# Parting two accumulations, moving a table add to TensorE, and joining maxima over two banks, in an attention and gated MLP kernel

## The chip, the cores and the metric

The kernel runs on one core of one Trainium2 chip. Its time is the device time of one execution in microseconds (us), as a median of runs. A profile of one execution gives each engine's instructions: TensorE (PE, and PEld for its weight loads), VectorE (DVE), ScalarE (ACT), GpSimd (POOL) and the DMA issues of SyncE (SP).

## The reference

Windowed attention with a linear bias by distance, for 8 batches of 8 heads, 576 positions and 64 columns a head, followed by a gated MLP over the 512 joined columns:

```
scores = scale * q @ k.T + slope[h] * -abs(i - j)    # kept where 0 <= i - j < 128, else -1e9
attn   = softmax(scores);  x = attn @ v
h = relu(x @ w_in);  u, v = h[:, :512], h[:, 512:]
v_n = layer_norm(v);  v_s = w_spatial @ v_n + b_spatial
out = (u * v_s) @ w_out
```

## The kernel before

Heads are taken in pairs (p = 0 to 3). The program first lists its operations (`plan.add`, and `plan.either` where two engines may do one), each with what it reads and writes. The string `PLACES` gives each operation a rank, three hexadecimal digits, by which each engine's queue is ordered; the instructions are then written out in that order, and every engine works through its queue in order.

**Batch 0 and half of batch 1** go through `turned`. PE makes first scores in two groups (tiles 0, 1, 2 and tiles 3, 4), each in two of four PSUM banks, `s`, one bank a head. DVE adds the bias table and takes each row's maximum in one instruction for each head and tile (line 765), ten for a pair. The maxima are turned by PE (line 783) into a bank `m`, and copied to `row`. Then PE makes the scores again, transposed, with table and maxima added by products with an identity and with ones (line 795); ACT takes exponentials (line 815); PE multiplies by v (line 824) into the two banks `x`; line 851 and 852 make the reciprocal of the sums; line 856 (DVE) or 862 (ACT) scales; line 869 turns the result back into `x`; lines 464 and 881 write it as a high and a low half, `xt`. The next pair's line 824 needs both `x` banks free.

**The MLP** of a batch (`gated`) is made of units of PE work that take the two banks `m` in turn: five v units (lines 1083 and 1105, twelve products each over four chunks of the contraction, chunk c being pair c's `xt`), then u, mixing (line 1155) and output units. A v unit is followed by a layer norm on DVE and POOL. The weights come as 64-bit floats in loads and DVE operations in the first 100 us; `mixing_weights` prepares the spatial weights, with a product for their largest column sum that takes both banks `m` (line 528), and comes in the list before the v units. `column_scale` is the helper for that product.

**Idle products.** Where the planner's model finds PE idle in the first 110 us, `emit` writes products whose result nobody reads (`fill`, line 391), 192 columns into the second `x` bank.

```
fills = int((now - idle) / (82 * (1 + low))) + 2 * (now < 30000)
```

Of the kernel before, what the change touches and what calls it, by code (L numbers as in the profile page):

```python
# [16 lines left out]
ALU = mybir.AluOpType  # L17
# [4 lines left out]
def _as_f32(bits):  # L22
# [9 lines left out]
    "00000500300200a01601a00600400c09c1e900902000701901b04800b04a03b05f03506005308005608200100d01101303102e05505904304201501c01d02202502a02802d"  # L32
    "03203403903d09d04404104505c06204d05105705e06c07207507818d1991a018b1a41a600800e00f01201001401701e01802302601f02402902c03702102702b03003302f"
    "03a03804704e05205d06306504f05b06606a07103603e04004603f04904c06803c04b05005a05805406406707607b07e08508908d07c08408809209306106906e06b06f074"
    "07707a06d07007308308707908c08e0980a20af0b80bc0c00a40b00b30b50b907d08108a0990970910a30a00c70cc0d20d60de0e40d00d90db0e00e207f09009609ba9a086"
    "0940aa0ba09e0c60ac0ae0e30b10c20bf0bb0b70c90c11430cf0cb0d70dc0e60eb0ef0f20f81cd11c12315415c13f14410b0f70c50ca0ce0d40da1021050e90f60fa0fd101"
    "10710f1130ff10c11011511b11e12b1300ea0f00fc0fe10310d10e10a11811d12112a12f13413611211712512919413513912e13212613a13e14715015716216913313b141"
    "14514b14f15315915e16816314615214d15b13c14014815117617f15816015f16a16717416f17917e19316116416c17317b1851781871801881a81b518919519f1a71cc1ae"
    "1a91b91bf1b41ba1c91c31d519019e1ad1b819d1b21aa1b71c01c71b61c11bc1cb1f020e1c61d61ed2051d11de1ef1e31f220720c1ec1fe20b1fa20d22920a21f224227221"
    "23324722c23d25223e24c25a25425e34f25927034708b08f0f30f509509a09f0a50ab0b60a70bd0c40e80ec0ee1f60f90a10a80b40a90a60ad0b20be0c30c80cd0d30d50d1"  # L40
    "0dd0e10fb10010611612012d10911111912212c0d80ed0df0e70e50f10f410410811411a12412711f12813113814a14c1551ea20218a19119b1f420613713d15617214915d"
    "16b18315a17516e17a16617714216d17d14e16517018217117c1841921961981ac1b31a11a519719a19c1a21db1d41dd1bd1ce1cf1da1d21e21af1d31f818118618e1d71a3"
    "1d91e71e81c81dc18c1b018f1ab1b11e51e61d81e11d01df1e01e41eb1ee1f11fb1fc2011f51fd1f91ff1f31f721320f21621121721b21e21821c21521a234200208219240"
    "24423f2421bb2041c22091c521d1be23b24825626c26f2774891c420321022021422622a22f23023822222822e23522d23122522b21222323223923c24125025324924f246"
    "24d24e25124324b26226326725826126026426626825525b27c23623a24a25725d25c25f27926527627d28328c29129629927528528a28f29229729b29f2a52a92ac28029e"
    "2a02a42aa2b02b42b929c2b12d02e02e42e82eb2ed2a72bd2d52dc2e12e72e92ec36f2b82c42bf2cf2c92d72d32ee2db2fc2f130233633d2ff30a30631633933b31031e346"
    "34d31b32c32534535735b33035534c36239739a35936c3a53a936537739137237e3a83ab37a3893953833a23af38c3a63aa3ac3a73b33cf3ae3bd3dc3b73d13e63c23e049d"
    "3d83e94a21ca23726b27a26a27e26927227428727128627828927328426e28226d27f27b28b28e2902942982a32a62a12a229329529a29d2bb2ab2b32a82b22ad2b52b72bc"
    "2af2b62d224528128828d2c22d92c62e22c02c82cb2d62c52d12ca2d82c72da2cd2df2ce2dd2c12cc2de2e32c32d42e62ea2f62fb2ef2f22f92fd2f02f52f42f830d303309"
    "30530b30831130730f30130e3242ae2ba2be2e531733231533431a31f32832f32a33132232731831d31331932932d31432332632b31c32133533a34234834434b33e34133c"  # L50
    "33f34034336934e35334a35135235635035435c36e3802f32fe2fa30c30431230033333835d38e3933995e92f732032e33738d38f39039236636d35a35f360363374375371"
    "37336736b35e36136a37036436837637837b37c37d38237f38438538838738a38138639d39e3a139639f39839c39b3a33a03a43b634937938b3943b13c73bb3c43fc3e13f2"
    "40040340740a40c40f3f03fa3fe40b40e41041241441741a4193f541141341641841b41d41e40141c42542a43143743a43d41542242c42f43443843b4414b841f428426432"
    "42d43943644243e44e44645348a48e45145c4564644a04a646146c4a54a94674784714944a84aa47d4a34994ac4e74eb4a74b74ea4ee4b24c14cf4be4cd4f44f94c94d44e9"
    "4d14e05044d94f34f84fb4e34fa50a50051052f5085155335145325f851c5365fb3be3c03b93c83b03b83c93cd3c53ce3b23b53ba3c33bf3ca3c13c63bc3cc3d03d23d33d5"
    "3d43d73d63da3d93dd3db3de3ee3e53eb3e23e83e33ea3e43ed3e73ef3ff3583ad3b43cb4044083f83fb4064303fd42e3f44233f342040242b3f94244054273f7421409433"
    "3f642943543c43f44344444844044544a44c44744b45a45445f45245845745d45946045545b4703df3ec3f140d46947f46b48446a47247347546846f47447747647a481485"
    "47b48047947c47e48346646d48848b49149649a4a148f49249349849549b4bc48d49049c4a449749e4ad4c34b04c64d644945e44d46245046548248748c4af4e14fc501727"
    "44f46346e4864e54e84e44e64b44b64c44c84bf4c54ba4c04bb4c24cb4cc4b14b94b54bd4c74ca4ae4b34ce4d04d84de4d54dd4d24d74da4df4d34db4f24f14f74f64fe4fd"
    "4ff4ec4f04ef4f551249f4dc4e24ed51852250d51f54f53554655155655955d56056254254c55055e56156356556756a56b56d54856456656956c56e57057255456f575577"  # L60
    "57a57f58258556857357957b57d5805845875f657157657457c57858157e58658358e58a5935c35c959059a5955a45ca5ce59e5ae5d05d55a75b75b05c25d15d75be5cd5c7"
    "5d96146285d45f561962b5de5fe61d5f961261863160260d62361762c64762462e63363763263f64863d65666865566468766066e74466a68a74a50550b507511521523502"
    "50651d52051b51e50c51950950f50e51651351a52552652852b52752952a52d52e53152c53054053853b53753c53953e53a54153d5435524ab50351752455555754554754b"
    "58855b59254a58955858c54958f55c59655359154d58b54e58d55a5945975985a05a25a35a559d5a159959c59b59f5b85a95ac5ba5bf5b55bc5b25b95ad5af5d253453f544"
    "55f5c55e05c15e25bb5d65c45da5c65dd5cc5df5c05d85b15c85b65d35b35cb5db5e15b45cf5e45e65f05f45e75ea5e85ed5ec5ef5ee5f26075fd60160960e60460860660a"
    "6006036295a65bd5ab5e35eb5f35f15f75fc64564b67267789e5aa5a85dc5e563063962f63560f61361c62161661b61e62661a61f62262a62062761161560c61060560b62d"
    "63463663c63b64363a64063863e64264465164964c65365764f65264a64e64d65066f5fa5ff62564665c66c65a66668867468968b69169769c6a46a768e69b69f6ae6b26b5"
    "6b86bb6bd6be6c06986ab6b96bc6bf6c16c36c56a36c26c76c96cc6d06d56dc6b06c66ca6cd6d26d76de6e47606c46cb6c86d36ce6da6d86e16df6ec6e76f77307366f2701"
    "6fb70c73c74370571774b74e71072171a72974d75072574872d75478d79174f75f79079475a76a77676777479279777177b78f77778579578079b79f7a27887a17af7a77b5"
    "7d47ad7bb7dc7ba7d78987c27de89c67567665465865b65f67167365e66266366d66166b65966566967065d66767867a68468668068368268567c67f67e68169d694699696"  # L70
    "69a68c68f6926956906936ac64167967b67d6a86aa6a16a56b66e36a26d46a96d16b16d96b76e56b36dd6b46e06af6d66ad6db6a66cf6e86e96eb6ef6ed6f46ea6f16f06f9"
    "6f36f870d70470870b71270770a6fe70370970f72468d69e6a06ba72f73472e73270271171971c71571871d72071371671f72271b71e6ff70e72372670671472b731733739"
    "73573b73a73f73e74173773d76474674974274c74074775176e75576277c6e26e66ee6f66f56fa6fc70072a75878a7a37a89e96fd72872c73878b78e78978c75675c763769"
    "76676b75275776876d75b76175d76577077275975e76c76f77377578378677977e77878477d78277a78179d79679979c7a07987a579a79e7a47a67b774577f7877937c17c8"
    "7b67c67f67da7ec7f97fc8008038058087e97f37f780480780980b80d8108138127ee80a80c80f8118148168177fa81581f82682a83083383780e81b82382882d831836838"
    "8a481882181e82b82583282e83983584483c84987e88284684f84b85988b89085685d88f89685b86986288089189786e88d88589a8c48ce8928a08d48d889d8ae8bd8a68b7"
    "8e68ea8b18c18dd8ba8c98ed8c68e58e88eb8cf8e18ee8ec8f890b8f28fd9109069179e39139249e57b47be7b27b97a97ac7c37c77c07c47ae7b37c57c97b17bf7ab7b07b8"
    "7bc7cb7cc7d57d87d07d37cd7cf7ce7d17d27d67e77db7e37e27e87df7e47e07e67dd7e17f87537aa7bd7ca7eb7ed7fd7ff7f181c7fe8277f281a7ef81d7f081980282c7f5"
# [42 lines left out]
class Plan:  # L121
# [69 lines left out]
    def order(self, links, due, clocked, phase=0):  # L191
# [12 lines left out]
        while events or any(ready.values()):  # L204
# [8 lines left out]
            for e, heap in ready.items():  # L213
                if heap and free[e] <= now:
# [8 lines left out]
                    else:  # L223
# [1098 lines left out]
```

## Time and profile before

| | |
|---|---|
| median of 3 runs | 550.73 us (549.65 to 551.71) |
| profiled execution | 549.54 us, span 547.8 us, 1.7 us lie around the span |
| PE busy | 535.9 us, 98% of the span, idle products included |
| DVE busy | 450.1 us, 82% |
| ACT busy | 388.5 us, 71% |

A busy PE is not PE at its best: ends of products are modelled, and idle products count as busy. The share of an engine is an average over a start, in which loads, weights and the first batches are prepared, and a long steady part.

### The profile page before, as it was taken

How to read it: one execution, taken by the hardware profiler on the slowest of the kernel's cores; microseconds unless marked ns; L12 is line 12 of the kernel's file. 1: busy time of each engine (PE TensorE's matmuls, PEld its weight loads, DVE VectorE, ACT ScalarE, POOL GpSimd, SP SyncE). 2: the span in 40 equal slices, each digit the busy share in tenths (PEclk: the TensorE clock that was granted, in tenths of full speed). 3: DMA queues.
4: the chain of work that ended last, by engine and by line, in shares of the span. 5: the costliest groups of instructions: out<-in, count | busy, mean ns of one | idle time of the engine just before them, and what ended most of it. 6: DMA issues, size and time to landing. Idle time of an engine off the chain costs nothing.

```text
span 547.8 us, 19213 instructions
## 1 busy us (share of the span) xinstructions
PE 535.9 (98%) x7756; PEld 396.3 (72%) x7759; DVE 450.1 (82%) x1644; ACT 388.5 (71%) x1213; POOL 60.3 (11%) x124
## 2 busy tenths in 40 slices
PE   9898999999999999999999999999999999999997
PEld 7787577875588857886678757886678757784775
DVE  8877999999998899688995899779997699725540
ACT  7576798998987797568874898579877687423212
POOL 1020220202110002100310010100210011001000
PEclk9999999999999999999999999999999999999999
DMA  8869331389979975968478786869364774510002
GB/s 247 310 201 320 96 104 59 82 161 241 193 156 222 193 144 129 223 104 191 108 151 182 143 189 133 193 133 196 104 124 119 150 89 89 88 66 23 2 12 75
DMA packets 161405, 78.67 MB, mean 144 GB/s; under 512 B 124834, under 2 KB 155554, under 8 KB 161316
## 3 DMA queue, kind: packets, MB, share of 16 engines
q1 hardware_dynamic: 161316, 77.45, 62.8%
q8 instruction: 60, 0.98, 0.8%
q14 instruction: 29, 0.24, 0.1%
HBM read 37.13 MB, written 9.44 MB: 85 GB/s over the span
## 4 chain that ended last, share of the span: by engine, by line
PE 80%; DVE 11%; DMA 3%; ACT 2%; issue 1%; SPq 1%; POOL 1%; ACTq 0%; DVEq 0%; POOLq 0%
PE m L1155 20%; PE m L1187 16%; PE m L1134 15%; PE m L1083 10%; PE s L724 6%; PE x L998 6%; PE m L1105 2%; DMA out_dram<-o 1%; DMA vb<-in_v_dram 1%; PE x L824 1%; PE s L795 1%; PE x L391 1%; DVE st L1044 1%; DVE vt L1057 1%; DVE staged L1094 1%
## 5 line engine op out<-in xcount | busy, mean ns | idle before, releaser
L922 ACT ACTIVATE prob<-prob,stat 128x192 f32<-128x192 f32 (+1 forms) x260 | 109.2, 423 | 11.3 <-DVE stat L916 10.9
L1155 PE MATMUL m<-wsp,staged 128*128 128x288 f16 x768 | 112.8, 286 | 0.0
L1134 PE MATMUL m<-xt,win 128*128 128x288 f16 x768 | 100.2, 286 | 1.5 <-ACT vt L468 1.5
L1187 PE MATMUL m<-gs,wout 128*128 128x288 f16 x768 | 99.4, 286 | 0.0
L954 ACT ACTIVATE pq<-prob,stat 128x192 f16<-128x192 f32 (+1 forms) x260 | 88.1, 420 | 11.3 <-issue 3.7
L1134 PEld LDWEIGHTS <-win 128*128 128x128 f16 x768 | 74.9, 98 | 22.7 <-issue 2.9
L1155 PEld LDWEIGHTS <-staged 128*128 128x128 f16 x768 | 74.5, 98 | 21.0 <-issue 2.2
L959 DVE SCALAR_TENSOR_TENSOR pq<-prob,stat,pq 128x192 f16<-128x192 f32 (+1 forms) x260 | 87.0, 379 | 2.9 <-ACT pq L954 2.5
L1187 PEld LDWEIGHTS <-wout 128*128 128x128 f16 x768 | 74.3, 98 | 20.5 <-issue 2.0
L916 DVE CUSTOM_DVE_ANT_0 prob<-s,tab 128x192 f32<-128x192 f32 (+1 forms) x260 | 71.3, 318 | 20.0 <-PE s L724 19.8
L1083 PE MATMUL m<-win,xt 128*128 128x512 f16 x384 | 86.6, 379 | 0.8 <-ACT o L1193 0.8
L1083 PEld LDWEIGHTS <-xt 128*128 128x128 f16 x384 | 36.2, 98 | 46.1 <-issue 5.5
L1053 POOL TENSOR_TENSOR st<-st,nhalf 128x1 f32<-128x1 f32 (+1 forms) x40 | 29.7, 742 | 296.4 <-DVE st L1049 288.1
L724 PE MATMUL s<-qkraw 64*64 64x64 f32 (+1 forms) x1116 | 52.7, 313 | 0.0
L1163 DVE TENSOR_TENSOR u<-m,u 128x288 f32<-128x288 f32 x64 | 28.9, 451 | 28.4 <-PE m L1155 28.1
L922 ACT ACTIVATION_READ_ACCUMULATOR prob<-prob,stat 128x1 f32 (+1 forms) x260 | 49.4, 190 | 0.0
L468 ACT ACTIVATE u<-m 128x288 f32<-128x288 f32 x60 | 24.3, 405 | 30.4 <-PE m L1134 30.3
L1193 ACT ACTIVATE o<-m,am 128x288 f32<-128x288 f32 x32 | 15.9, 499 | 41.2 <-PE m L1187 31.0
L724 PEld LDWEIGHTS s<-qkraw 64*64 64x64 f32 x1116 | 40.8, 133 | 2.0 <-issue 1.2
L998 PEld LDWEIGHTS <-vh 128*64 128x64 f16 (+1 forms) x1664 | 34.4, 111 | 8.7 <-issue 7.2
L998 PE MATMUL x<-moved,vh 128*64 128x64 f16 (+1 forms) x1664 | 39.2, 196 | 0.0
L998 PE MATMUL x<-moved,vl 128*64 128x64 f16 (+1 forms) x832 | 37.5, 195 | 0.0
(167 smaller groups left out, 761.4 us busy)
## 6 DMA issues: line engine op xcount, KB each, us to landing
qkraw<-in_qk_dram SPq DMA_DIRECT2D x28, 576.0 KB, 4.2
vb<-in_v_dram SPq DMA_DIRECT2D x32, 320.0 KB, 6.0
out_dram<-o SPq DMA_DIRECT2D x64, 144.0 KB, 2.1
staged<-in_w_in_dram SPq DMA_DIRECT2D x8, 512.0 KB, 7.1
moved<-in_w_out_dram SPq DMA_DIRECT2D x4, 512.0 KB, 6.3
gw<-in_w_spT_dram SPq DMA_DIRECT2D x4, 288.0 KB, 6.0
moved<-pq SPq DMA_TRANSPOSE x52, 4.8
qkraw<-in_qk_dram SPq DMA_DIRECT2D x2, 320.0 KB, 5.2
```

The source lines that it names most:

```text
L724: nc.tensor.matmul(sc[j]()[out, at:at + k1 - k0], raw()[rows, 0, i * D:(i + 1) * D], raw()[rows, 1, k0:k1], start=True, stop=True, skip_gr ...
L916: nc.vector.tensor_tensor_reduce(pt(), sc[t][j]()[:m, SOFF[t]:SOFF[t] + n], tabs[h]()[:m, W - n:], -0.125, 3e38, ALU.add, ALU.min, st()[:m ...
L922: nc.scalar.activation(pt(), pt(), AF.Exp, bias=st()[:m, NM, j, t:t + 1], scale=-1.0, accum_out=st()[:m, SM, j, t:t + 1])
L954: nc.scalar.activation(pq[j]()[:m, 0, qs], prob[2 * (p % 2) + j]()[:m, cs], AF.Copy, scale=st()[:m, RC, j, t:t + 1])
L959: nc.vector.scalar_tensor_tensor(pq[j]()[:m, 1, qs], prob[2 * (p % 2) + j]()[:m, cs], st()[:m, RC, j, t:t + 1], pq[j]()[:m, 0, qs], ALU.mu ...
L998: nc.tensor.matmul(xp()[j * D:(j + 1) * D, x0:x0 + D], l()[rows, kt, j * D:(j + 1) * D], rhs, start=(i % 2, j) not in seen, stop=False, sk ...
L1053: nc.gpsimd.tensor_tensor(st()[:m, 11:12], st()[:m, 10:11], nhalf()[:m], ALU.pow)
L1083: nc.tensor.matmul(pt(), xt[c]()[:, X0[a] + t * P:X0[a] + (t + 1) * P], win()[:, c, w, DH:DF], start=(n == 0), stop=(n == 3 * NC_ - 1))
L1134: nc.tensor.matmul(pt()[:, :HS], win()[:, c, w, d * P:(d + 1) * P], xt[c]()[:, X0[a] + hf * HS:X0[a] + (hf + 1) * HS], start=(n == 0), sto ...
L1155: nc.tensor.matmul(pt()[:, :HS], l, r, start=(n == 0), stop=(n == len(ops) - 1))
L1163: nc.vector.tensor_tensor(u(), pt()[:, :HS], u(), ALU.mult)
L1187: nc.tensor.matmul(pt()[:, cs], wout()[:, d, w, e * P:(e + 1) * P], gs[d]()[:, a, cs], start=(n == 0), stop=(n == 3 * ND - 1))
```

## The change

Seven edits, and a new order string.

1. `v_unit` takes its contraction in parts. For the first two v units of batch 0 the parts are chunks 0 and 1, chunk 2, chunk 3, each an operation of its own with its own reads; the bank stays open between them.
2. For batch 0, `scored` adds the bias table to the first scores on PE, by a product of an identity with the table for each head and half tile (18 for a pair). DVE then takes plain maxima over both heads' banks at once, in three instructions for a pair: tile 0, tiles 1 and 2, tiles 3 and 4. For this the four `s` banks become one tensor. The maxima now come with the other sign, so `row` is multiplied by a new constant `less` (-1) in place of `ones`.
3. `mixing_weights` comes in the list after the first two v units, just before the third.
4. The bias row of the mixing weights is scaled with one instruction over two partitions, on DVE or ACT, and one on one partition, in place of three on one partition each.
5. The two DVE instructions of lines 851 and 852, and those of lines 1048 and 1049, become operations of their own.
6. Idle products: half as many after 5 us and no two extra ones, in the first bank of `x1`, `m1`, `m0` that the plan shows quiet; none where no bank is quiet.
7. `rest` takes two `s` banks instead of one where its tag is `s`. A constant `nident` is made; the branch that would use it, `LOWER`, has no members.

The diff, without the order string and the definitions of new constants:

```
-                                fills = int((now - idle) / (82 * (1 + low))) + 2 * (now < 30000)
+                                fills = int((now - idle) / ((82 if now < 5000 else 164) * (1 + low)))
...
+        for n, k, z, start, *_, fills in out:
+            if fills:
+                bank = next((b for b in FILLED if quiet(b, free, start)), None)
+                if bank or start < 5000:
+                    self.fill(fills, bank=bank or FILLED[0])
...
+    OPEN = (0, 2), (2, 3), (3, 4)
+    ADDED = [(0, p) for p in range(4)]
+    LOWER = []
...
-    plan.kept["s"] = [ps.tile([P, 4 * P], F32, name=f"s{k}") for k in range(4)]
+    sbanks = ps.tile([P, 4, 4 * P], F32, name="s")
+    plan.kept["s"] = [sbanks[:, k] for k in range(4)]
...
-        def f():
-            for a in (64, 96):
-                nc.vector.tensor_scalar(r2()[a:a + 1, :], bt()[a:a + 1, :], sc(a, a + 1), None, ALU.mult)
-            nc.vector.scalar_tensor_tensor(r2()[96:97, :], bt()[96:97, :], sc(96, 97), r2()[96:97, :], ALU.mult, ALU.subtract)
+        def fv():
+            nc.vector.tensor_scalar(r2()[64:66, :], bt()[64:66, :], sc(64, 66), None, ALU.mult)
+        def fa():
+            nc.scalar.activation(r2()[64:66, :], bt()[64:66, :], AF.Copy, scale=sc(64, 66))
+        def f():
+            nc.vector.scalar_tensor_tensor(r2()[64:65, :], bt()[64:65, :], sc(64, 65), r2()[64:65, :], ALU.mult, ALU.subtract)
...
+        for x in range(len(TILES[t])):
+            for j in range(2):
+                rows = slice(j * D, (j + 1) * D)
+                nc.tensor.matmul(sc[j]()[x * D:(x + 1) * D, off:off + n], identb()[rows, rows], tabs_[j]()[rows, W - n:],
+                                 start=False, stop=True, skip_group_check=True)
...
+                    if added:
+                        nc.vector.tensor_reduce(ms()[:m, t:t + z, :, 0], sbanks[:m, a:a + 2, SOFF[t]:SOFF[t] + z * n].rearrange("p j (t n) -> p t j n", n=n), AX.X, ALU.max)
+                        return
...
-        def v_unit(t):
+        def v_unit(t, cuts=((0, NC_),)):
+            for c0, c1 in cuts:
+                def f(c0=c0, c1=c1):
+                    for c in range(c0, c1):
+                        for n, (a, w) in enumerate(PASS):
+                            nc.tensor.matmul(pt(), xt[c]()[:, X0[a] + t * P:X0[a] + (t + 1) * P], win()[:, c, w, DH:DF], start=c + n == 0, stop=c == NC_ - 1 and n == 2, skip_group_check=len(cuts) > 1)
...
+            v_rem() if t == NQ - 1 else v_unit(t, OPEN if b == 0 and i < 2 else ((0, NC_),))
...
+        if t == 4:
+            mixing_weights(FIRST + 8000, late)
-    mixing_weights(FIRST + 8000, late)
```

The order string holds 2,715 ranks before and 2,765 after, one for each operation of the list. Some of them, in the order of the changed string (hexadecimal):

| operation of PE (unless named) | rank before | rank after |
|---|---|---|
| pair 0, times v (L824) | 47 | 39 |
| pair 1, times v | 76 | 6a |
| pair 2, transposed scores, first group (L795) | 73 | 70 |
| DVE: low half of the first two chunks of w_in for v (L548) | ba | 9c |
| pair 2, turned back (L869) | b3, b8 | ac, b0 |
| v unit 0 | e9 | b2, d5, ee |
| pair 3, times v | c7 | be |
| v unit 1 | ff | c5, e1, f0 |
| mixing weights' column sums (L528) | dc | f7 |
| batch 1 pair 0, times v | fb | ff |
| v unit 2 | 10a | 105 |
| v unit 4 (64 rows) | 133 | 13d |
| first mixing unit (L1155) | 16f | 187 |

## Rows read from the trace of the kernel before

**Rows 1.** The page: busy time of the engines, and the granted clock in 40 slices.
```profile
PE 535.9 (98%) x7756; PEld 396.3 (72%) x7759; DVE 450.1 (82%) x1644; ACT 388.5 (71%) x1213; POOL 60.3 (11%) x124
...
PEclk9999999999999999999999999999999999999999
```

**Rows 2.** Windows: length, then PE, PEld, DVE, ACT, POOL busy (count), clock, DMA.
```profile
13.00:40.00 27.00, 25.53 (x684) 21.78 (x679) 21.18 (x82) 17.28 (x38) 4.81 (x11) 1.00 0.78 255
40.00:57.30 17.30, 14.85 (x277) 11.60 (x268) 14.16 (x47) 12.71 (x30) 0.42 (x2) 1.00 0.94 313
57.30:126.00 68.70, 68.58 (x952) 50.23 (x953) 67.40 (x223) 62.49 (x186) 11.67 (x24) 1.00 0.42 98
126.00:150.00 24.00, 22.19 (x253) 13.55 (x252) 22.43 (x79) 20.99 (x67) 6.07 (x10) 1.00 1.07 226
...
480.00:500.00 20.00, 19.19 (x227) 13.25 (x225) 4.85 (x12) 5.30 (x11) 0.55 (x1) 1.00 0.18 61
```

**Rows 3.** Windows of the idle products alone (line 391): PE and PEld busy.
```profile
13.00:40.00 27.00, 2.56 (x25) 2.09 (x25) 1.00 0.78 255
40.00:57.30 17.30, 4.95 (x48) 4.08 (x48) 1.00 0.94 313
```

**Rows 4.** Timeline of PE: start, length, instructions, idle before and its releaser.
```profile
1.34 3.22 PE L391 MATMUL x<-ones 128*128 128x192 bf16 x19 [1.34 <-DVE ones L410]
...
26.08 1.98 PE L391 MATMUL x<-ones 128*128 128x192 bf16 x22 [0.67 <-DVE xt L881]
...
41.73 0.74 PE L391 MATMUL x<-ones 128*128 128x192 bf16 x7 [1.38 <-ACT prob L862]
...
44.42 1.98 PE L391 MATMUL x<-ones 128*128 128x192 bf16 x22 [0.92 <-DVE xt L881]
...
54.16 0.65 PE L528 MATMUL m<-wsp,ones 128*128 128x288 bf16 x4
...
57.28 2.75 PE L1083 MATMUL m<-win,xt 128*128 128x512 f16 x12
```

**Rows 5.** Chain that ended last, in order of time: start, length, what.
```profile
39.53 2.16 ACT prob L862 x10
...
57.45 2.59 PE m L1083 x12
```

**Rows 6.** Timeline of DVE.
```profile
16.85 0.23 DVE L765 CUSTOM_DVE_ANT_0 s<-s,tab 64x64 f32<-64x64 f32 x1 [0.73 <-PE s L724]
...
19.74 0.21 DVE L851 TENSOR_SCALAR sm<-x,am 128x6 f32<-128x6 f32 x1
...
24.04 0.21 DVE L765 CUSTOM_DVE_ANT_0 s<-s,tab 64x64 f32<-64x64 f32 x1
...
25.62 0.41 DVE L881 TENSOR_TENSOR xt<-x,xt 128x256 f16<-128x256 f32 x1
...
39.84 0.22 DVE L765 CUSTOM_DVE_ANT_0 s<-s,tab 64x64 f32<-64x64 f32 x1
...
44.29 1.27 DVE L548 SCALAR_TENSOR_TENSOR win<-wx,ham,win 128x1024 f16<-128x1024 f32 x1
...
56.10 0.81 DVE L531 TENSOR_REDUCE wam<-m 128x1 f32<-128x288 f32 x2
```

**Rows 7.** DVE groups by line and shape: count, busy us, mean ns, idle before.
```profile
L531 DVE TENSOR_REDUCE ham<-m 128x1 f32<-128x512 f32 x2 | 1.4, 680 | 0.0
...
L641 DVE TENSOR_SCALAR r<-moved,wam 1x576 f16<-1x576 f32 x2 | 1.0, 515 | 0.1
L642 DVE SCALAR_TENSOR_TENSOR r<-moved,wam,r 1x576 f16<-1x576 f32 x1 | 0.8, 817 | 0.0
...
L531 DVE TENSOR_REDUCE wam<-m 128x1 f32<-128x288 f32 x2 | 0.8, 448 | 0.0
```

**Rows 8.** Timeline of PE: sixteen score products, and eight products with ones.
```profile
24.54 0.88 PE L724 MATMUL s<-moved 64*64 64x192 f32 x16
...
28.21 0.34 PE L795 MATMUL s<-row,ones 64*64 64x192 bf16 x8
```

More of the change, by code (lines that the diff above doesn't have):

```diff
@@ L262, in emit, with quiet @@
         end, out = self.order(self.links(False), due, True)
-        for n, k, *_, fills in out:
-            self.fill(fills)
+        span = {n: (start, z, self.ops[n][0][k][0]) for n, k, z, start, *_ in out}
+        held = {bank: [(b.wide, [span[n] for n in b.users]) for b in self.tags[bank[0]] if b.at == bank[1]] for bank in FILLED}
+        def quiet(bank, t0, t1):
+            for wide, users in held[bank]:
+                if wide and users[0][0] <= t1 and max(z for _, z, _ in users) >= t0:
+                    return False
+                if any(e != "PE" and a <= t1 and z + 150 >= t0 for a, z, e in users):
+                    return False
+            return True
+        free = 0
+        for n, k, z, start, *_, fills in out:
[3 more added lines that the diff above has]
+                    self.fill(fills, bank=bank or FILLED[0])
+            if self.ops[n][0][k][0] == "PE":
+                free = z
             self.ops[n][0][k][2]()
@@ L351, in attn_gmlp_kernel @@
     ones = fixed([P, W], BF16, "ones")
+    less = fixed([P, D], BF16, "less")
+    nident = fixed([P, P], F16, "nident")
     masked = fixed([P, D], BF16, "masked")
@@ L387, in attn_gmlp_kernel, with fill @@
     relf, relT = (plan.buf(work, "u", 7, [P, W], F32) for _ in range(2))
-    def fill(n, start=False):
+    plan.kept["m"] = [ps.tile([P, 4 * P], F32, name=f"m{k}") for k in range(2)]
+    def fill(n, start=False, bank=("x", 1)):
         for _ in range(n):
-            nc.tensor.matmul(plan.kept["x"][1][:, 5 * D:], ones()[:, :P], ones(), start=start, stop=True, skip_group_check=True)
+            nc.tensor.matmul(plan.kept[bank[0]][bank[1]][:, 5 * D:], ones()[:, :P], ones(), start=start, stop=True, skip_group_check=True)
     plan.fill = fill
@@ L415, in f @@
             nc.vector.memset(masked(), MASKED)
+            nc.vector.memset(less(), -1.0)
             nc.vector.memset(powers()[:, 0:1], 2.0 ** -13)
@@ L420, in f @@
             nc.vector.memset(nhalf(), -0.5)
-        plan.add("DVE", 370, 501, f, (), [(masked, 0), (powers, 0), (wpowers, 0), (nhalf, 0)])
+        plan.add("DVE", 430, 501, f, (), [(masked, 0), (less, 0), (powers, 0), (wpowers, 0), (nhalf, 0)])
         for k in range(2):
@@ L428, in constants @@
         plan.add("POOL", 720, 500, f, [(ident, 0)], [(ident, 0)])
+        plan.add("ACT", act(P), 2000, lambda: nc.scalar.activation(nident(), ident(), AF.Copy, scale=-1.0), [(ident, 0)], [(nident, 0)])
         plan.add("PE", 160, 0, lambda: fill(1, True), [(ones, 0)], [(masked, 0)])
@@ L523, in column_scale @@
         pts = [plan.buf(ps, "m", 2, [P, 512], F32) for _ in range(0, n, step)]
+        for pt in pts:
+            pt.wide = step > 5 * D
         def f():
@@ L712, in keys, with scored @@
         return max(0, i - 2) * D, (i + 1) * D
-    def scored(sc, t, off, raw):
+    def scored(sc, t, off, raw, tabs_=None):
         for x, i in enumerate(TILES[t]):
@@ L765, in f @@
                         nc.vector.tensor_tensor_reduce(at, at, tabs[2 * p + j]()[:m, W - n:], -1.0, 3e38, ALU.add, ALU.min, ms()[:m, t, j, 0:1])
-                plan.add("DVE", 2 * (dve(n) + 37 if n > D else dve(n) + 25), due + 500 + t * 300, f, [(x, 0) for x in tabs[2 * p:2 * p + 2]], [(sc[0], t), (sc[1], t), (ms, t)])
+                plan.add("DVE", dve(2 * z * n) + 40 if added else 2 * (dve(n) + 37 if n > D else dve(n) + 25), due + 500 + ts2[0] * 300, f,
+                         [] if added else TABS, [(sc[j], t) for t in ts2 for j in range(2)] + [(ms, t) for t in ts2])
         def split(e):
@@ L773, in rest @@
         def rest():
-            mp = plan.buf(ps, *tag, [P, 4 * P], F32)
+            mp, *spare = (plan.buf(ps, *tag, [P, 4 * P], F32) for _ in range(2 if tag[0] == "s" else 1))
             row = plan.buf(work, "row", 1, [P, S], BF16)
@@ L783, in f @@
                     nc.tensor.transpose(dst, upper()[:m, t].rearrange("p a b -> p (a b)"), identb()[:m, :m])
-            plan.add("PE", 366, due + 3000, f, MS + [MR, (ident, 0)], [(mp, 0)])
+            plan.add("PE", 366, due + 3000, f, MS + [MR, (ident, 0)], [(x, 0) for x in (mp, *spare)])
             copy(S, lambda: (row(), mp().bitcast(BF16)[:, :S]), due + 3300, [(mp, 0)], [(row, 0)], on_dve=380)
@@ L806, in f @@
                         for j, r in enumerate(half):
[L807 removed]
+                            mm(j, key % 2, col, k, sign()[r, :D], row()[r, q * D:(q + k) * D])
                     for key, q, k, col in PIECES[g]:
@@ L810, in f @@
                             mm(j, key % 2, col, k, raw()[r, 1, key * D:(key + 1) * D], raw()[r, 0, q * D:(q + k) * D])
-                plan.add("PE", (1100, 960)[g], due + 4000 + g * 700, f, ALL + [(row, 0), (ones, 0), (ident, 0)] + [TAB[2 * p + j] for j in range(2)],
+                plan.add("PE", (1100, 960)[g], due + 4000 + g * 700, f, ALL + [(row, 0), (sign, 0), (ident, 0)] + [TAB[2 * p + j] for j in range(2)],
                          [(x, 0) for x in tt], "SS")
@@ L868, in f @@
                         m = shape(t)[0]
-                        nc.tensor.transpose(xp()[:, at:at + m], xn()[:m, s], ident()[:m, :m])
+                        if (b, p) in LOWER:
+                            nc.tensor.matmul(xp()[:, at:at + m], xn()[:m, s], ident()[:m, :m], is_transpose=True, start=s == 0, stop=False, skip_group_check=True)
+                        else:
+                            nc.tensor.transpose(xp()[:, at:at + m], xn()[:m, s], ident()[:m, :m])
                         at += m
@@ L878, in rest, with f @@
                 copy(nb * D, lambda to=to, xv=xv: (to(0), xv()), d + 1200, [(xp, 0)], xh)
+                if (b, p) in LOWER:
+                    def f(to=to, xv=xv):
+                        nc.tensor.matmul(xv(), nident(), to(0), start=False, stop=True, skip_group_check=True)
+                    plan.add("PE", pe(nb * D), d + 1400, f, [(nident, 0)] + xh, [(xp, 0)], "FF")
+                    copy(nb * D, lambda to=to, xv=xv: (to(1), xv()), d + 1500, [(xp, 0)], xl)
+                    continue
                 def f(to=to, xv=xv):
```

176 lines of the change are left out of this document (97 added, 79 removed).

## Prediction, on record before the changed kernel ran

> **What bounds the kernel now.** I read the page first. PE is busy for 98% of the span at a granted clock of 1.00, the 2.4 GHz level, in every slice [rows 1]. That share says little, since idle products count in it, so the windows come next [rows 2]. From 57.3 us on PE stands still for 0.12 us in 68.7, then 1.81 in the next 24 and 0.81 around 490; nothing in the change adds or removes products there, so that part can only be begun earlier. DVE is busy for 67.40 of the same 68.7 us and ACT for 62.49: the stretch from 57.3 to 126 is tight on two engines, and the gain has to be worked out for both.
>
> Ahead of 57.3 the idle products alone are the third view [rows 3]. From 13 to 40 us PE idles for 1.47 us and spends 2.56 on them, a hole of 4.0; from 40 to 57.3 it idles for 2.45 and spends 4.95, a hole of 7.4. The timeline shows where [rows 4]: at 41.73 seven products after 1.38 us of standing still, at 44.42 twenty-two after 0.92. In both, and at 26.08, the wait ahead is one for a reader of the `x` bank into which the idle products write, so these can hold PE themselves. The v units, which could fill the hole, start only at 57.28, behind the column sums of the mixing weights at 54.16 that take both `m` banks first. The chain of waits says what sets the pace of the hole itself [rows 5]: times v, scaling (2.16 us on ACT for pair 2), turning back, two copies, and only then the next pair.
>
> **The change part by part.**
>
> **v units in parts, mixing weights behind them.** Twelve products of a v unit follow one another in 2.59 us [rows 5], 0.216 each. By the new ranks six and then three products of both units stand between pair 2's turning back and the mixing weights' column sums, among what ran from 44.42 to 57.28 [rows 4]; the last parts come straight after, still ahead of the column sums. So 18 products, 3.9 us, go into a hole of 7.4. For this the data must be there: the low half of the weights for chunks 0 and 1 is written at 44.29 before [rows 6], and its new rank puts it ahead of the ten maxima that began at 39.84 [rows 6]. Some 3 us of DVE work less ahead of it makes it ready by about 42. PE's side of this edit: -3.9, between 0 (the weights are late and PE waits inside the hole) and -5.2 (both units whole). Behind a part that waits for its chunk stand, in PE's queue, batch 1's scores, which DVE needs next; the wait is then theirs. The mixing weights are late next: their column sums move from 54.16 to behind the units, but the first mixing unit, which needs them, keeps a rank behind all v units and five u units.
>
> **Maxima.** Ten instructions with their reads of the accumulator run from 16.85 to 19.74, 2.9 us a pair [rows 6]. Three reductions over 128, 768 and 768 columns replace them. No row has 768 columns over two banks; the nearest are 512 columns in 680 ns and 288 in 448 [rows 7], so 1.04 ns a column: 945 ns for 768, 282 for 128. Two of 288 in a row took 0.81 us, not 0.90 [rows 6], so 0.09 is hidden each time, and a pair costs 2.0 us. That saves 0.95, 3.8 for four pairs. Bounds: nothing hidden saves 0.7 a pair; were the two-bank pattern at half the rate, a pair would cost 3.6 and lose 0.7. I take 0.95, since the rows are the same operation on the same memory. The Trainium skill (VectorE: DVE Perf Modes, Rules for kernel authors) calls tensor_reduce the slowest operation of this engine and would restructure it off a hot path. By that reading the edit gains nothing, and the total would be -0.5 in place of -4.3; no row here shows a column costing more in a reduction than about 1.04 ns.
>
> On the chain: pair 2's maxima stand ahead of pair 0's scaling at 19.74, and six of pair 3's ten run from 24.04 to 25.62 ahead of the low half that frees the `x` banks [rows 6]. In the new order only tile 0's reduction stays ahead of it. So the banks come free 0.95 + 1.58 - 0.2 = 2.3 us earlier, and pair 1's product with v, which now has a rank ahead of pair 2's transposed scores, can follow. PE's hole of 4.0 us ahead of 40 can give that.
>
> **Table adds on PE.** 18 products a pair. Eight such small products in a row took 0.34 us, of which one alone is most; sixteen f32 score products took 0.88 [rows 8]. So 0.3 to 1.0 us a pair; nearest in type is the first, and I take 0.35, 1.4 in all. Their cover is PE's holes and idle products; for pair 2 without cover they cost 0.35 on the chain, inside the rounding of the 2.3. No DMA is added.
>
> **Bias row.** Three instructions of 515, 515 and 817 ns [rows 7] become one of 515 and one of 817: -0.52 on DVE, or -1.03 if ACT takes the first.
>
> **Split operations, new constants, second `s` bank.** No instruction more or less; other work can stand between the halves. Taken as nothing. One memset and one copy of 128 columns come in the first 5 us, ahead of the first loads' data; nothing too. The spare bank makes a maxima turn of batch 1 wait for one more bank, at most one exponential, inside the hole.
>
> **Idle products halved.** The 48 of 40 to 57.3 give back nothing that the v units do not already take; the 22 at 26.08 cover 1.98 us and no longer wait for a reader. That is part of the 2.3 above. It costs nothing while the clock stays up.
>
> **The sum.** PE's side: -3.9 - 2.3 = -6.2. DVE's side: work saved -3.8 - 0.5 = -4.3, if its 9.0 us of standing still between 13 and 57.3 [rows 2] stay as they are. From 57.3 on both must come earlier by the same amount, so the smaller sets it: -4.3 on the profiled 549.54, 545.2. The runs' median is 1.2 above the profiled execution, so I give 546.4 for the median. A measurement of this kernel can tell about 0.5%, 2.75 us, from no change.
>
> **The rivals.**
>
> *More than that.* DVE's standing still was mostly waiting for products and for ACT, which come earlier too, and the second pair of w_in words for u is moved ahead of 57 us. Then PE's side holds: -6.2, or 8 with the 1.81 us at 126 to 150 cleared as well. Time 542.7 to 544.5. Against it: ACT has only 6 us to spare from 57.3 to 126, and less in its first half.
>
> *Given back.* The hole moves instead of closing: PE comes to 57.3 early and waits there for DVE and ACT, or the reductions are worth nothing. For it speaks DVE's 1.3 us of slack in 68.7. Time 548.0 to 550.7, say 549.5; with the rule on reductions 550.2.
>
> *Slower by the clock.* With half the idle products, and none where no bank is quiet, the clock could fall between 13 and 57 us. The first 19 idle products took 3.22 us and the 22 at 26.08 took 1.98 [rows 4], 0.17 against 0.09 each, which is what the slow level costs. PE has 9.9 us of other products from 40 to 57.3 [rows 2, 3]; at 1.2 GHz they take 9.9 more, the hole left beside the v units gives back 3.5, and 4.3 - 6.4 is 2.1 slower: 552.8. It decides from 7.8 us of such work on, and over 10.5 us the kernel is slower by more than can be missed. Against it: the clock is 1.00 through all of the gaps before, and the holes themselves shrink. The Trainium skill (TensorE: Matmul & The Clock Gate, Part 1: The HAM clock gate) has the slow level as the default that activity lifts and idleness brings back, which speaks against this edit; the slices before agree only so far that a busy PE kept 1.00.
>
> *Not what it says: the four banks as one tensor.* Idle products waited for readers of other columns in their bank [rows 4], so waits go by something coarser than columns. Were it the tensor, the second group's scores, in two other banks, would wait for the first group's maxima: 1.1 us for each of four pairs, and about 1.8 for each of batch 1's two pairs, which keep the old maxima: 8.0 in all, 3.7 more than is gained, 554.4. It decides from 4.3 us of such waits on. Against it: the row would show the same if waits go by bank.
>
> **How the numbers follow.** The forecast, -4.3 with its own range of 544.0 to 548.0, has 0.45; more than that 0.20; given back 0.20; the clock 0.08; one tensor 0.07. Faster by over 0.5% (under 548.0): the first two, and a little of the last two where they come in part, 0.68. Within 0.5%: all of given back, and half of what is left of the last two, 0.24. Slower: 0.08. The range of 541.8 to 550.2 leaves out the two slower cases and the far ends of the others, 2 in 10.
>
> **What the profile after would show.** The first product of a v unit near 43 us, and both units done before 54; idle products from 40 to 57.3 down from 48 to under 15. DVE's line of maxima for batch 0 gone, twelve reductions in its place at about 0.28 and 0.95 us. Pair 1's product with v some 2 us earlier, and ahead of pair 2's transposed scores. The stretch that began at 57.3 moved up by 4 to 5 us, with PE's gaps in it still under 1 us: gaps there mean that DVE or ACT gave the gain back. A granted clock under 1.00 in any slice, or waits of scores for reductions in other banks, would make me wrong on the slow side; a shift of six and more on the other.

## The result, and the profile after

| | time, median (runs) | against before, 95% interval |
|---|---|---|
| before | 550.77 us (549.65 to 551.71, 4 runs) | |
| changed | 557.62 us (556.91 to 558.10, 4 runs) | 1.0127 (1.0110 to 1.0145) |

The change makes the kernel 1.3% slower, some 7 us; 546.4 was forecast, and 557.6 lies over the range of 541.8 to 550.2. The profiled execution has a span of 555.9 us against 547.8.

The page of the changed kernel: busy time, and the granted clock in 40 slices.
```profile
PE 532.7 (96%) x7730; PEld 390.9 (70%) x7733; DVE 437.4 (79%) x1563; ACT 393.9 (71%) x1220; POOL 62.7 (11%) x124
...
PEclk9999999999999999999999999999999999999999
```
The digit 9 stands for 0.9 or more, and the windows below give 1.00, the 2.4 GHz level, as before [rows 2]; three of the four runs have a mean of 1.000, one 0.997. So the rival of the clock is not what happened to this kernel. DVE has 12.7 us less to do, more than the 4.3 that I summed (ACT has 5.4 us more), and the kernel is still slower.

Its windows, columns as in [rows 2].
```profile
13.00:40.00 27.00, 21.70 (x583) 17.80 (x587) 17.13 (x40) 12.48 (x29) 3.97 (x8) 1.00 0.64 213
40.00:57.30 17.30, 14.20 (x330) 10.38 (x320) 15.42 (x46) 12.11 (x29) 4.01 (x5) 1.00 0.88 298
57.30:126.00 68.70, 66.15 (x840) 46.74 (x841) 64.31 (x210) 60.76 (x172) 10.54 (x22) 1.00 0.47 116
...
150.00:480.00 330.00, 326.35 (x4768) 240.99 (x4767) 280.03 (x1084) 261.74 (x874) 33.84 (x62) 1.00 0.73 147
```
From 13 to 40 us, where my hole was to close, PE stands still for 5.3 us, and DVE (21.18 before [rows 2]) and ACT (17.28) have less done. All three engines stand still more than before: they wait for one another. PE's waits by line and releaser (us in total, times, longest) name it.
```profile
PE s L762 <- ACT prob L873: 3.3, 5, 0.8
PE s L841 <- POOL most L828: 2.5, 1, 2.5
...
PE s L853 <- ACT prob L873: 1.9, 2, 1.1
PE s L762 <- DVE most L818: 1.7, 1, 1.7
...
PE s L853 <- DVE most L818: 1.1, 1, 1.1
```
Score products (line 762) and transposed scores (853) wait for those who read `s`, exponentials (873) and reductions (818): 3.3 + 1.9 + 1.7 + 1.1 = 8.0 us. The 2.5 us before line 841 are another matter: there the turn of batch 1's maxima waits for its own operand, which line 828 splits. Whether these read the same banks, the timelines of PE, DVE and ACT tell. A pair's first group uses banks 0 and 1, its second 2 and 3.
```profile
9.33 0.33 PE L762 MATMUL s<-qkraw 64*64 64x64 f32 x4 [1.67 <-DVE most L818]
...
22.70 0.98 PE L853 MATMUL s<-qkraw 64*64 64x192 f32 x19
...
25.30 0.36 PE L853 MATMUL s<-gs,ident 64*64 64x64 bf16 x12 [1.05 <-ACT prob L873]
...
27.55 0.33 PE L762 MATMUL s<-moved 64*64 64x64 f32 x4 [0.66 <-ACT prob L873]
...
45.42 1.47 PE L1158 MATMUL m<-win,xt 128*128 128x512 f16 x6
```
```profile
7.26 2.01 DVE L818 TENSOR_REDUCE most<-s 64x2 f32<-64x128 f32 x3 [1.18 <-PE s L770]
...
23.71 0.96 DVE L818 TENSOR_REDUCE most<-s 128x4 f32<-128x768 f32 x1 [1.33 <-PE s L853]
```
```profile
24.70 0.54 ACT L873 ACTIVATE prob<-s 128x448 f32<-128x448 f32 x1 [4.52 <-DVE most L818]
...
28.80 0.49 ACT L873 ACTIVATE prob<-s 128x384 f32<-128x384 f32 x1 [1.30 <-PE s L770]
```
At 9.33 pair 1's first group (banks 0, 1) starts only as the third reduction of pair 0 ends (7.26 + 2.01), which reads banks 2 and 3. At 25.30 the second transposed group waits for an exponential of the first (24.70 + 0.54). It goes the other way too: the reduction at 23.71, of the second group, stands 1.33 us until transposed scores into banks 0 and 1 are through (22.70 + 0.98), and the exponential at 28.80, of a second group, waits for the table adds of the next pair's first. Readers and writers of different banks take turns, which is the last of my rivals, and waits of scores for reductions in other banks are the sign that I named for it. The v units' first product comes at 45.42, not near 43, behind such waits.

### The profile page after: what moved, and what is told of

The parts are those of the page before. It is cut to its first block, busy times and chain, and to the rows that moved or that the text cites. A ratio compares the mean times of both kernels' runs of the same rounds, so it can differ in the third digit from the quotient of the medians.

```text
span 555.9 us, 19083 instructions
## 1 busy us (share of the span) xinstructions
PE 532.7 (96%) x7730; PEld 390.9 (70%) x7733; DVE 437.4 (79%) x1563; ACT 393.9 (71%) x1220; POOL 62.7 (11%) x124
## 5 line engine op out<-in xcount | busy, mean ns | idle before, releaser
L1127 POOL TENSOR_TENSOR st<-st,nhalf 128x1 f32<-128x1 f32 (+1 forms) x40 | 31.4, 785 | 289.4 <-DVE st L1123 281.1
L762 PE MATMUL s<-qkraw 64*64 64x64 f32 (+1 forms) x1116 | 54.5, 315 | 4.7 <-ACT prob L873 2.0
L1271 ACT ACTIVATE o<-m,am 128x288 f32<-128x288 f32 x43 | 21.4, 498 | 45.0 <-PE m L1265 35.2
L499 ACT ACTIVATE u<-m 128x288 f32<-128x288 f32 x55 | 22.3, 405 | 22.1 <-PE m L1212 21.7
```

The lines of the kernel that those rows point to most:

```text
L762: nc.tensor.matmul(sc[j]()[out, at:at + k1 - k0], raw()[rows, 0, i * D:(i + 1) * D], raw()[rows, 1, k0:k1], start=True, stop=True, skip_gr ...
L1127: nc.gpsimd.tensor_tensor(st()[:m, 11:12], st()[:m, 10:11], nhalf()[:m], ALU.pow)
```

## The experiments

Ratios are against the kernel before on the same chip. Four theories appear in the expectations. T: the four banks as one tensor. O: the new order and the parted units. C (once I): the new rule for idple products. S: the split operations. Runs that change tensors or idle products alone keep the order of every queue. Runs that change the list of operations let the planner place other work anew, so they show an edit together with its order.

**One tensor.** Two tensors of two banks keep the three reductions:
```
-    sbanks = ps.tile([P, 4, 4 * P], F32, name="s")
-    plan.kept["s"] = [sbanks[:, k] for k in range(4)]
+    sbanks = [ps.tile([P, 2, 4 * P], F32, name=f"s{k}") for k in range(2)]
+    plan.kept["s"] = [sbanks[k // 2][:, k % 2] for k in range(4)]
...
```
*Changed kernel, two tensors.* 

> The changed kernel with the four s banks as two tensors of two banks each; the three reductions over two banks, the order string and all else stay. Theory T (one tensor makes scores wait for readers of other banks): in the changed kernel's profile PE stands still before score products (lines 762, 853, 841) for some 10 us ahead of 62 us, most of it behind a reader of another pair of banks. Those waits go, the first product of the third v unit comes 3 to 6 us earlier than at 68.3, and the time falls by 3 to 8 us, to 550 to 554.6. Theory O (the new order, with v units in parts and column sums moved, is what costs): waits change their name, the time stays within 1.5 us of 557.6.

*Changed kernel, four tensors, a reduction for each head.* 

> The changed kernel with four s tensors of one bank each, so that each reduction over two banks becomes two over one (six for a pair in place of three). Theory T: as with two tensors, 550 to 554.6, plus the fixed share of 12 more reductions, up to 0.15 us each on DVE, at most 1.8 us, of which part is hidden. That joining over two banks by itself is worth much: then this is over 2 us slower than with two tensors. Theory O: 557.6 or a little more.

*Kernel before, its four banks made one tensor (the two lines with a minus above, nothing else).* 

> The kernel before, with only the four s banks made one tensor; its ten maxima, its order string and all else stay. Theory T: scores, transposed scores and exponentials wait for readers in other banks, as in the changed kernel; the time rises by 3 to 10 us, to 554 to 561, with PE waits on ACT exponentials and DVE maxima before score products that the kernel before does not have. Theory O: the same as before, 550.7 within 1.5.

| run | median | ratio |
|---|---|---|
| changed, two tensors | 550.20 | 0.9993 (0.9966 to 1.0020) |
| changed, four tensors | 548.98 | 0.9983 (0.9956 to 1.0010) |
| before, one tensor | 570.61 | 1.0351 (1.0301 to 1.0400) |

T holds from both sides, and beyond its own bound on the kernel before, whose order had never been laid around such waits: +3.5%. Not all of that is these waits: idle products wait there too, and the granted clock fell in that kernel, to 0.96 from 13 to 57.3 us. On the changed kernel one tensor costs 1.0127 / 0.9993, 1.34% or 7.4 us, give or take 1.8 (both intervals). PE's waits in the two-tensor kernel, then in the kernel before with one tensor:
```profile
PE m L1213 <- ACT vt L499: 1.8, 4, 0.6
PE m L1234 <- issue: 1.8, 3, 1.0
PE s L842 <- POOL most L829: 1.7, 1, 1.7
```
```profile
PE s L796 <- DVE most L766: 6.1, 3, 2.6
PE x L392 <- DVE xt L882: 4.4, 2, 2.8
PE s L725 <- ACT prob L816: 2.6, 4, 0.9
PE s L725 <- DVE most L766: 2.0, 2, 1.4
```
With two, no score product waits for an exponential or a reduction any more; with one on the old order 10.7 us of exactly these appear. Four tensors do no worse than two, 1.2 us less with intervals that overlap, so joining a reduction over two banks is not shown to be worth anything. DVE's reductions, PE's first v products and pair 1's product with v in the two-tensor kernel, then the last of these before:
```profile
L819 DVE TENSOR_REDUCE most<-s 128x4 f32<-128x768 f32 x8 | 7.3, 940 | 0.0
...
L819 DVE TENSOR_REDUCE most<-s 64x2 f32<-64x128 f32 x4 | 1.1, 282 | 1.0 <-PE s L770 1.0
```
```profile
25.08 1.88 PE L883 MATMUL x<-vb,prob 128*64 128x65 f32 x64
...
39.30 1.47 PE L1159 MATMUL m<-win,xt 128*128 128x512 f16 x6
```
```profile
29.30 1.88 PE L824 MATMUL x<-vb,prob 128*64 128x65 f32 x64
```
The rest of the change now does what I said of it in the start: pair 1's product with v comes 4.2 us earlier than before, the v units from 39.30 on. This profile is of the fastest of ten runs, 547.65 us at a mean clock of 1.000. The median is that of the kernel before, where I had 4.3 us less. The other runs look for these.

One place to look is the clock of each run. Only two of the ten runs with two tensors, and five of ten with four, had a mean of 0.999 or more; of the kernel before on the same chip fifteen of nineteen had. At like clocks the changed kernel is ahead: at 0.996 and 0.997 seven runs with two tensors have a median of 550.22, four of the kernel before 552.46; at 0.999 and 1.000 the two runs with two tensors took 547.65 and 550.19, the five with four tensors have a median of 548.45, the fifteen of the kernel before one of 549.97. So 1 to 2 us of the missing 4.3 seem to have gone with the clock. Runs sorted afterwards are no experiment, and these are few.

**Undoing the two terms of the sum**, on two tensors (the notes behind # are not in the code, and the ranks change with the list).
```
-    OPEN = (0, 2), (2, 3), (3, 4)        # whole units
+    OPEN = (0, 4),
...
-    ADDED = [(0, p) for p in range(4)]   # maxima as before
+    ADDED = []
```
*Whole v units.* 

> The changed kernel with two s tensors, its first two v units whole again (each at the place of its last part); maxima, table adds, idle products and order stay. My step 'v units in parts' says the 18 products that lie in holes are PE's side of the gain: undone, PE has 3.9 us more to do after the hole, the last of the five v units comes 2 to 4 us later than with two tensors (70.8 in that profile) and the time rises by 2 to 4 us over it. Rival (the maxima carry the gain, PE has holes anyway): within 1 us of it.

Measured: 552.85, 1.0044 (1.0017 to 1.0070): 2.8 us over two tensors, give or take 2.1. The parts are worth about what the term says (3.9), at least 0.7. None of its ten runs reached a clock of 0.998, but the seven at 0.996 or 0.997 have a median of 552.13 against 550.22, so most of this is not the clock. In its profile the last v unit begins at 78.8 us, 8.0 later and not 2 to 4, at a granted clock of 0.94 from 13 to 40 us.

*Maxima as before.* 

> The changed kernel with two s tensors, but batch 0's maxima as in the kernel before: ten instructions of DVE for a pair that add the table and take the maximum, no table adds on PE, ones in place of the negated row. v units stay in parts. My step 'maxima' says DVE's side of the gain is 3.8 us: undone, the time rises by 2.5 to 4 us over two tensors. Rival (PE's side alone sets the gain): within 1 us of it.

Measured: 550.97, 1.0005 (0.9978 to 1.0031): 0.7 over two tensors, give or take 2.0. The expected rise of 2.5 reaches only the edge of that; 3.8 is out. Here too the clock differs: six of these ten runs had 0.999 or more, against two of ten. The four at 0.996 or 0.997 have a median of 552.39 against 550.22, so the maxima may be worth some 2 us that the clock takes back.

*Old order.* 

> The changed kernel with two s tensors, whole v units, the mixing weights ahead of them in the list, and every operation in the order of the kernel before: what is left of the change is the table adds, the maxima over two banks, the bias row and the fewer idle products. If the maxima are what DVE's side needed, the chain gets 2.3 us shorter without any new order: 1.5 to 3 us faster than the kernel before. If the reductions are worth nothing where the order is not made for them: within 1 us of before.

Measured: 549.88, 1.0000 (0.9978 to 1.0022): no gain. What the maxima alone bring, this does not tell. The kernel also holds the halved idle products and the split operations, which the expectation left out, and each of these made the kernel before slower (1.0085 and 1.0174, below).

*New start, old tail.* 

> The changed kernel with two s tensors, in its new order for the first 1,000 operations (to about 180 us) and in the order of the kernel before from there on. With two tensors the profile stands 3.2 us ahead of before at 200 us and 0.9 at 440, the rest lost to waits of PE in mixing and u units that the old order has not. If the new order of the steady part loses it: the time is 1 to 2 us under that of two tensors, and the span ends about 3 us ahead of before. If the split operations or the missing slack lose it: no difference.

Measured: 550.99, 1.0001 (0.9973 to 1.0030), no gain over two tensors. That does not clear the new tail, since the old tail's ranks were made for another list.

**Idle products as before**, in five of these kernels:
```
-    fills = int((now - idle) / ((82 if now < 5000 else 164) * (1 + low)))
+    fills = int((now - idle) / (82 * (1 + low))) + 2 * (now < 30000)
...
-    if bank or start < 5000:
-        self.fill(fills, bank=bank or FILLED[0])
+    self.fill(fills, bank=FILLED[0])
```
*Changed kernel.* 

> The changed kernel with the idle products as before: one for each 82 ns and two more, all in the second x bank. Theory T and theory O: within 1.5 us of 557.6, since the granted clock is 1.00 in every slice of the changed kernel with few idle products. Theory I (the products that are missing cost something): the time falls by 2 us or more.

*Two tensors.* 

> The changed kernel with two s tensors and the idle products of the kernel before (one for each 82 ns and two more, all in the second x bank). With two tensors and halved idle products, eight of ten runs had a mean granted clock of 0.994 to 0.997, and the kernel before is at 1.000 in most. Theory C (the halved idle products let the clock fall in the start, 0.003 of 546 us at half speed being some 3 us of stretch and 1.5 to 2 lost): the clock is 1.000 in nearly all runs and the median falls to 547.5 to 549. Rival (the clock falls whatever the idle products): 550.2 within 0.7, clocks as they were.

*Four tensors.* 

> The changed kernel with four s tensors (six reductions for a pair) and the idle products of the kernel before. Theory C: 547.5 to 548.5 and clocks of 1.000; with two tensors the same within 1 us, since waits by pair of banks cost little. Rival: 549.0 within 0.7.

*Old order.* 

> The order of the kernel before, whole v units, two s tensors, and the idle products of the kernel before: of the change only the table adds, the maxima over two banks, the bias row and the split operations are left. My step 'maxima' (3.8 us of DVE work saved, the chain shorter by up to 2.3) would make it 1.5 to 3 us faster than the kernel before even in the old order. If it only moves the waits: within 1 us of before. Theory C: the granted clock, 0.990 to 0.997 in most runs of the same kernel with halved idle products, is 1.000 here.

*Old tail.* 

> Two s tensors, the idle products of before, the new order for the first 1,000 operations and the order of before from there on. If the new order of the steady part costs 1 to 2 us, this is that much under the same kernel with the new order throughout, 546 to 547.5. If any steady part loses that much when it begins early (DVE and ACT have nothing to spare): the same within 0.7.

Measured: 556.95 (1.0110), 549.59 (0.9986), 550.68 (1.0009), 557.42 (1.0135), 552.43 (1.0024). In the new order the rule makes no difference in time that shows. It does in the clock with two tensors: nine of twelve runs have 0.999 or more, where two of ten had; with four it is seven of twelve and five of ten. So half of theory C holds there, and the time does not follow. In the old order, with the table adds, the old rule is 1.35% slower than the new one (1.0135 against 1.0000, intervals 1.0106 to 1.0164 and 0.9978 to 1.0022). PE's waits there give about half of these 7.4 us, a wait of 3.6: an idle product in the second `x` bank holds PE behind the scaling of `prob`.
```profile
PE x L418 <- ACT prob L922: 3.6, 1, 3.6
```

**The rule for idle products, and the split, on the kernel before.**

*New rule.* 

> The kernel before, with only the new rule for idle products: half as many after 5 us, none where no bank is quiet, in the first quiet bank of x1, m1, m0. Theory C (fewer idle products let the clock fall): most runs at a mean clock of 0.990 to 0.998, and the time 1 to 3 us over before. My step (costs nothing while the clock stays up; the idle product at 26.08 no longer waits for a reader): the same as before or up to 1 us faster, clocks of 1.000.

*As many as before, in quiet banks.* 

> The kernel before, with as many idle products as before, but only where a bank is quiet and in that bank. If the number is what keeps the clock: within 1 us of before, or up to 1.5 us faster since no idle product waits for a reader of the second x bank (1.6 and 1.4 us of such waits before). If those left out where no bank is quiet are what counts: 2 to 5 us slower with clocks of 0.990 to 0.997, as with the halved number (554.8).

Measured: 554.82, 1.0085 (1.0058 to 1.0113); and 547.78, 0.9942 (0.9922 to 0.9962). The two halves of edit 6 have opposite signs. Windows of the first, then its page's clock; then a window of the second and its idle products by line.
```profile
40.00:57.30 17.30, 14.01 (x226) 9.59 (x228) 13.54 (x43) 12.08 (x28) 1.31 (x2) 0.85 0.97 307
```
```profile
PEclk9998799999999999999999999999999999999999
```
```profile
40.00:57.30 17.30, 16.78 (x297) 12.78 (x290) 15.94 (x58) 13.11 (x31) 2.27 (x4) 1.00 1.01 334
```
```profile
L415 PE MATMUL x<-ones 128*128 128x192 bf16 x77 | 9.5, 280 | 1.3 <-DVE ones L434 1.3
...
L415 PE MATMUL m<-ones 128*128 128x192 bf16 x60 | 6.1, 246 | 0.0
```
Halved, the clock goes to 0.85 in the window of the hole. In full, in quiet banks, it stays at 1.00, 137 products are written, and none but the first waits, where three waited for readers of `x` before [rows 4]. This version, the kernel before with only the bank of its idle products chosen, beats both the kernel before and the changed one.

*Split operations.* 

> The kernel before, with only the layer norm's and the reciprocal's pairs of DVE instructions as operations of their own, the second half at the next rank. Theory S: 1 to 2.5 us slower than before, with PE's waits of u units at 0.7 to 0.8 us where before has one of 0.24. Rival: within 0.8 us of before.

*Joined again, two tensors.* 

> The changed kernel with two s tensors, the two DVE instructions of the layer norm and those of the reciprocal of the sums joined into one operation again, at the rank of the first. Theory S (between the halves DVE takes other work, the layer norm ends later, a v unit's bank is freed later, and a u unit of PE waits 0.3 to 0.8 us for it in most batches): the waits of u units for ACT's copies of v units shrink, and the time falls by 1 to 2.5 us, to 548 to 549. Rival (these waits come from starting early with nothing to spare): within 0.8 us of 550.2.

*Joined, idle products as before.* 

> As the run before, and the idle products of the kernel before. Theory S: 1 to 2.5 us under the same kernel with the halves split (549.6). Rival: within 0.8 of it.

Measured: 559.61, 1.0174 (1.0140 to 1.0208); 554.63, 1.0095 (1.0067 to 1.0122); 553.59, 1.0080 (1.0051 to 1.0109). Splitting on the old order is slower and joining on the new one is slower as well. The page of the split kernel and its waits:
```profile
PE 539.0 (97%) x7784; PEld 398.0 (72%) x7787; DVE 449.1 (81%) x1656; ACT 386.2 (70%) x1195; POOL 60.2 (11%) x122
```
```profile
PE x L392 <- ACT prob L866: 3.4, 1, 3.4
PE x L392 <- DVE xt L885: 2.7, 2, 1.9
PE m L1141 <- ACT vt L469: 2.4, 4, 0.8
```
In the kernel before, the last of these reads:
```profile
PE m L1134 <- ACT vt L468: 1.5, 3, 0.9
```
ACT has 18 instructions fewer than before and DVE 12 more [rows 1 give 1,213 and 1,644]: with other operations in the list the planner gives other work to each engine, and idle products then wait 3.4 us for ACT, where it was 1.4 [rows 4]. S is not shown: u units wait 2.4 us behind a v unit's copy against 1.5 before, and the longest wait is no longer, 0.8 against 0.9. What the three runs have in common is a list other than the one that the ranks were made for, and a cost of 1 to 2%; that the ranks are the cause is the likely reading, not shown apart from the edits.

*Four tensors, full number in quiet banks.* 

> The changed kernel with four s tensors and six reductions for a pair, its idle products in quiet banks but as many as before (one for each 82 ns and two more). Its runs with halved idle products lay at 547.7 to 549.4 where the granted clock was 1.000 and at 551.6 to 552.7 where it was 0.993 to 0.997. If the number keeps the clock up: 547.7 to 549, faster than before by 0.2 to 0.4%. If the clock falls as often as before: 549 to 550.5, no difference.

Measured: 549.50, 0.9980 (0.9962 to 0.9999), and five of twelve runs at 0.999 or more. A window of its profile:
```profile
40.00:57.30 17.30, 14.44 (x237) 9.56 (x230) 13.89 (x49) 13.37 (x31) 1.27 (x2) 0.90 0.97 309
```
The number alone does not keep the clock up in the new order, and a gain is not shown beyond the interval's edge.

## Why the prediction was wrong, step by step

**The tensor.** The step that failed is the chance of 0.07 for *four banks as one tensor*. The mechanism was as written there: waits go by tensor, and joining the four banks cost 7.4 us, give or take 1.8, for which the sum has no term. The price written there, 8.0 us, came near by luck. I had put all of it on scores behind maxima, which are 2.8 us of the 8.0 in PE's waits; the other 5.2 stand behind exponentials, which I did not list. Against it I held that waits could as well go by bank; the diff joins four tensors that had been separate, and the row shown fitted both readings, so it gave no reason to put the rival this low. Readers also wait for writers elsewhere (23.71, 28.80), which I did not list either.

**The sum without the tensor.** It forecast -4.3 and 0.9993 was measured: at most 0.34%, 1.9 us, at the interval's end. Three steps of it fell or stand open.

*The smaller side sets it.* The maxima were sized rightly: 940 ns for 768 columns and 282 for 128, against 945 and 282 forecast. The saving was summed a little high, since 2.9 less 2.0 is 0.9 for a pair and 3.6 in all, not 0.95 and 3.8. But undoing them costs 0.7 us, give or take 2.0, while undoing the parts costs 2.8. DVE's work alone did not set the gain; how much of it the clock hides is open. No gain is also what I drew from the Trainium skill (VectorE: DVE Perf Modes, Rules for kernel authors), which calls tensor_reduce the slowest operation of this engine. The rows here do not show it slow: between the two sizes a column costs (940 - 282) / 640 = 1.03 ns, as in the rows before [rows 7], and in the instruction that it replaced (384 - 237) / 128 = 1.15 ns.
```profile
L765 DVE CUSTOM_DVE_ANT_0 s<-s,tab 128x192 f32<-128x192 f32 x48 | 15.8, 384 | 0.0
...
L765 DVE CUSTOM_DVE_ANT_0 s<-s,tab 64x64 f32<-64x64 f32 x12 | 2.4, 237 | 0.8 <-PE s L724 0.7
```

*Idle products halved cost nothing while the clock stays up.* On the kernel before it does not stay up, and the halving costs 1.4% (1.0085 against 0.9942), close to the rival's mechanism. In the changed kernel the clock held, with 39 idle products; what held it there is not settled. With two tensors and the same 39, eight of ten runs have a mean of 0.994 to 0.997. The page that I cited (the Trainium skill, TensorE: Matmul & The Clock Gate, Part 1: The HAM clock gate) has idleness bring the slow level back. The 0.85 agrees, but the changed kernel, where PE stands still for 5.3 and 3.1 us of the two windows up to 57.3, kept 1.00. My price of the slow level rests on no row of it: from 1.30 to 4.60, where the first 19 idle products took 0.17 us each, the granted clock is 1.00.
```profile
1.30:4.60 3.30, 3.22 (x19) 2.72 (x19) 1.00 0.67 197
```
The other part of that step, that idle products no longer wait for a reader, was right and worth 0.6% on the kernel before.

*Split operations as nothing.* Not so on the kernel before, where the edit and what the planner made of it cost 1.7%; in the new order, made for the split, it can't be told apart. How much of it is the order, how much the split, stays open.

**v units in parts.** Right in mechanism, 2.8 (give or take 2.1) in place of 3.9, and the first product at 39.30 once the tensor was parted.

**Given back.** Of the gain in the start some is lost later. The rows of the products of the 64-row v units give the start of batch 0's first and of the last batch's last one, before, with two tensors and with four, each in one profile:
```profile
L1105 PE MATMUL m<-win,xt x96: 377/379/403, 74.3 to 498.5; 128*64 128x512 f16 x96
```
```profile
L1184 PE MATMUL m<-win,xt x96: 377/380/404, 70.8 to 496.5; 128*64 128x512 f16 x96
```
```profile
L1183 PE MATMUL m<-win,xt x96: 378/380/404, 72.4 to 496.5; 128*64 128x512 f16 x96
```
With two tensors 3.5 us of lead become 2.0; with four it is 1.9 and 2.0, and nothing is lost. What loses it stays open: the run with the old tail did not cure it, and part of the waits (1.8 us of mixing units) has no releaser in the profile.

## What to carry to other kernels

Making one tensor of several, so that one instruction may span them, also joins their waits: cut it no wider than that instruction (two banks here, not four), or leave it out where, as here, one instruction for each bank does no worse. A hand-tuned order seems to belong to its list of operations; an edit taken out or put in alone measures the order too, so test it from both sides and trust the runs that leave the queues alone. Work that only keeps the clock up should write where nobody reads. A cost that is said to be nothing while the clock stays up needs the clock of every run, not of one profile.

## What was not expected of the hardware

In the same 17.3 us PE was busy for nearly the same time at different clocks: 14.20 us at a granted clock of 1.00 in the changed kernel, 14.01 us at 0.85 in the kernel before with halved idle products. It is not the same work, 330 products against 226, of other kinds, and the share before it differs too: the first had stood still for 5.3 us of the 27 before, the second for 2.5. So these rows do not tell what made the clock fall.
